# Last wo of a decode attention kernel: the fourth row of every partition is brought ahead of the last v, by four strided transfers to 64 partitions

## The chip, the cores and the metric

The kernel runs on one core of a Trainium2 chip. The metric is the device time of one execution in microseconds, as the median of several runs. Engines are named as the profile names them: PE (matmul, with PEld for its weight loads), DVE (vector), ACT (scalar), POOL (GpSimd) and SP (the queue that issues nearly all transfers). Behind SP and ACT stand 16 DMA engines that move the bytes.

## The reference

One decode step of a parallel block: with `xn = layernorm(x)` for 8 rows of 512, the output is `x + attention(xn) + mlp(xn)`, in float32.

```python
q = (x @ wq).reshape(B, Sq, Hq, Dh).transpose(0, 2, 1, 3)      # 32 heads of 128
k = jnp.repeat(k_cache, rep, axis=1)                           # 8 kv heads, 8192 keys
scores = jnp.einsum("bhqd,bhkd->bhqk", q, k) * (Dh ** -0.5)
o = jnp.einsum("bhqk,bhkd->bhqd", softmax(scores), v)
attention = o.transpose(0, 2, 1, 3).reshape(B, Sq, Hq * Dh) @ wo   # wo: 4096 x 512
mlp = einsum(mish(xn @ w1 + b1), w2)                               # 512 -> 1792 -> 512
```

K and V caches are 256 MiB each, so nearly all of the time is reading them once.

## The kernel before

**Packs.** The 8 kv heads are taken in 4 pairs (PAIRS) and the 8 batches in pairs, which gives 16 packs p of two batches b. Each (p, b) needs one block of K (`kT`) and one of V, 8 MiB each: 128 partitions of 64 KB. Scores of a pack are computed while V of the pack before is multiplied.

**Places and the queue.** All large loads go through three fixed areas of on-chip memory, `place`: "a" (16 rows of 1024 columns a partition; V, and w1 at the start), "b" (20 such rows; K, at the end V of the last pack's first batch and w2) and "w" (4 rows; wq and wo). `plan` (L114) appends a load to `queue`; `pump` (L103) issues loads from the head of this queue while the area that the next one wants is free, and `release` (L110) frees an area. So the order of loads is the order of the `plan` calls, SP (L121) issues them in that order, and a load that waits holds up all behind it. K alternates between rows 0 to 15 and 4 to 19 of "b" (`up`, L142); the last kT lies in rows 4 to 19.

**wo.** wo is laid out in 4 parts of 2 MB, one for each pair of kv heads: 128 partitions with 4 rows (OR = 4) of 1024 columns, 4 KB a row. The first three are used inside the loop (`outputs`, L530). The last one is used in the tail and is loaded in two halves between the pieces of w2.

**Order of loads at the end** (L175 to L181): V of the last pack, batch 0, to "b"; V of batch 1 to "a", in three quarters and one quarter; then w2 in four pieces to "b", with half of the last wo after the second and after the third piece.

**The tail** (L695 to L721). `merges`, `turning` (L498, a selecting matrix from the identity), `values` (L454, V times probabilities) of batch 0, `gather` (L468), `sums`, `merge` (L484), `add_up` (L545: starts the sum of the final output in PSUM), `keep_busy(4)` (L636: matmuls whose result nobody reads), `values` of batch 1, then `gather`, `down` (L623: w2 products) of the first piece, `merge`, and `turn` (L507). `turn` spreads the heads' outputs with four matmuls (L514) so that partition and row fit the layout of wo, and copies the result from PSUM to `oW` in four copies, by DVE (L528) and ACT (L526) in turn. Then follow, on PE in this order: `down` of the second piece, `last_outputs` (L556) of wo's rows 0 and 1, one `keep_busy` matmul, `down` of the third piece, another, `last_outputs` of rows 2 and 3, `down` of the fourth piece. Each float32 matmul stands in the trace as two records. DVE copies the result (L720) and SP stores it (L721).

The instructions of PE, DVE and POOL run in the order of the code (the loop at L725 pins it). Waits between engines are set by what the instructions read and write. Completion of transfers is counted on eight semaphores that SP's transfers use in turn, so the ninth transfer waits for the landing of the first where nothing has implied this already.

Of the kernel before, what the change touches and what calls it, by code (L numbers as in the profile page):

```python
# [8 lines left out]
F32 = mybir.dt.float32  # L9
# [4 lines left out]
P = 128  # L14
B = 8
# [8 lines left out]
G = 4  # L24
# [3 lines left out]
BW = 1024  # L28
# [10 lines left out]
PAIRS = HKV // 2  # L39
NP = B // PB  # L40
PACKS = PAIRS * NP
R = P // G
HE = P // 2
# [7 lines left out]
KR = DH * 2 * NB // P  # L51
# [12 lines left out]

QR = CC
OR = 4
W1R = 2 * CC * P // P
W2R = G * FT // 2 * FP // P
FAR = 1e38
# [3 lines left out]
def kernel(  # L73
# [12 lines left out]
    nc = tc.nc  # L86
# [3 lines left out]
    work = ctx.enter_context(tc.tile_pool(name="work", bufs=2))  # L90
# [4 lines left out]
    place = {n: const.tile([P, size], F32, name=f"kv{n}") for n, size in sizes.items()}  # L95
    queue = []
    taken, landed = {}, {}

    def rows_of(blocks):

        return blocks.rearrange("j p f -> (j p f)").rearrange("(p f) -> p f", p=P)
# [12 lines left out]
    def plan(what, at, blocks, parts=((0, 1),), lo=0):  # L114

        rows = rows_of(blocks)
        n = rows.shape[1]
        t = place[at][:, lo : lo + n]

        def load(cols):  # L120
            nc.sync.dma_start(t[:, cols], rows[:, cols])  # L121
            return t

        for first, end in parts:
            cols = slice(round(first * n), round(end * n))
            queue.append((what, at, lambda cols=cols: load(cols)))


    sc = const.tile([P, 512], F32, name="sc")
# [7 lines left out]
    def blocks_of(src, p, b):  # L137
        i, k = divmod(p, NP)
        lo = ((k * PB + b) * HKV + 2 * i) * NB
        return src[lo : lo + KN]  # L140
# [10 lines left out]
    def plan_v(p, b, at, parts=((0, 1),)):  # L151
        plan(("v", p, b), at, blocks_of(v, p, b), parts)

    def plan_wq(i):
        plan(("wq", i), "w", wq[i * CC : (i + 1) * CC])

    def plan_wo(i, parts=((0, 1),)):
        plan(("wo", i), "w", wo[i * 4 : i * 4 + 4], parts)


    plan_wq(0)
    plan("w1", "a", w1)
# [4 lines left out]
    for p in range(PACKS):  # L167
        for b in range(PB):
            plan_k(p, b)
            if (p, b) in between:  # L170
                what, i = between[p, b]
                (plan_wq if what == "wq" else plan_wo)(i)
            if p > 0:
                plan_v(p - 1, b, "a")
    plan_v(PACKS - 1, 0, "b")  # L175
    plan_v(PACKS - 1, 1, "a", ((0, 3 / 4), (3 / 4, 1)))
    W2_PARTS = ((0, 2), (2, 4), (4, 6), (6, 7))
    for k, (lo, hi) in enumerate(W2_PARTS):
        plan("w2", "b", w2, ((lo / W2R, hi / W2R),))
        if 0 < k < 3:  # L180
            plan_wo(PAIRS - 1, (((k - 1) / 2, k / 2),))  # L181


    S = psum.tile([P, GK], F32, name="s")
# [5 lines left out]
    ident = const.tile([P, P], F32, name="ident")  # L190
# [29 lines left out]
    aT = const.tile([P, 2 * W2R, Q], F32, name="aT")  # L220
    xw = aT.rearrange("p j q -> p (j q)")[:, : W1R * 2 * B]
    xw = xw.rearrange("p (r t b) -> p r t b", r=W1R, t=2)

    def setup():
# [33 lines left out]

        wide = scratch[:B, 2 * D : 2 * D + W1R * P]
        for t in range(2):  # L260
            nc.gpsimd.tensor_copy(
                wide.rearrange("b (r c t i) -> b r c t i", r=W1R, c=CC, t=2)[:, :, :, t, :],
                xc.rearrange("b (c i r) -> b r c i", c=CC, r=W1R),
            )
# [26 lines left out]
    def setup_w1(wide):  # L291
        for r in range(W1R):
            nc.tensor.transpose(  # L293
                M[:, 64 + r * B : 64 + (r + 1) * B], wide[:, r * P : (r + 1) * P], ident[:B, :B]
            )
        for t in range(2):
            nc.vector.tensor_scalar(
                xw[:, :, t, :],
                M[:, 64 : 64 + W1R * B].rearrange("p (r b) -> p r b", r=W1R),
                half[:, t : t + 1],  # L300
                None,
                op0=ALU.mult,
            )

        nc.gpsimd.memset(pt, 0.0)
# [148 lines left out]
    def values(b, vt, lo=0, hi=ROUNDS):  # L454


        for k in range(lo, hi):
            for c in range(G):
                j = G * k + c
                nc.tensor.matmul(  # L460
                    O[b][Q * c : Q * (c + 1), :],
                    pt[:, b, j % 2, j // 2].rearrange("p t e h -> p (t e h)"),
                    vt[:, W4 * DH * j : W4 * DH * (j + 1)],
                    start=(k == 0),
                    stop=(k == ROUNDS - 1),
                )
# [15 lines left out]
    oT, oW = {}, {}  # L482

    def merge(p, b):  # L484

        i, k = divmod(p, NP)
        at = 168 + b * 2 * REP
        nc.tensor.matmul(M[:, at : at + 2 * REP], OS.pop((p, b)), hsel, start=True, stop=True)  # L488
        if b == PB - 1:
            if k == 0:  # L490
                oT[i] = work.tile([P, 2, REP, B], F32, name="oT")
            nc.vector.tensor_mul(  # L492
                oT[i][:, :, :, k * PB : (k + 1) * PB].rearrange("p e h b -> p (e h) b"),
                M[:, 168 : 168 + PB * 2 * REP].rearrange("p (b r) -> p r b", b=PB),
                RT.pop(p).rearrange("p b e h -> p (e h) b"),
            )

    def turning():  # L498

        tid = work.tile([P, HT * KINDS * P], F32, name="e", bufs=1)[:, : OR * P]  # L500
        tid = tid.rearrange("p (r g i) -> p r g i", r=OR, g=G)
        nc.vector.tensor_copy(
            tid, ident.rearrange("p (i r o) -> p r o i", r=OR, o=1).to_broadcast([P, OR, G, Q])
        )
        return tid

    def turn(i, tid):  # L507


        to = oW[i] = work.tile([P, OR, 2, B], F32, name="oW")  # L510
        o = oT.pop(i).rearrange("p n h b -> p (n h b)")
        cols = 2 * REP * B
        for r in range(OR):
            nc.tensor.matmul(  # L514
                M[:, 256 + r * cols : 256 + (r + 1) * cols],
                tid[:, r].rearrange("p g i -> p (g i)"),
                o,
                start=True,
                stop=True,
            )  # L520
        m = M[:, 256 : 256 + OR * cols].rearrange("p (r j q) -> p j r q", r=OR, j=G)
        for j in range(G):
            rows = slice(Q * j, Q * (j + 1))
            dst = to[rows].rearrange("p r h b -> p r (h b)")
            if i == PAIRS - 1 and j % 2:
                nc.scalar.copy(dst, m[rows, j])  # L526
            else:
                nc.vector.tensor_copy(dst, m[rows, j])  # L528

    def outputs(i, w):  # L530

# [24 lines left out]
    def last_outputs(lo, hi, w):  # L556

        for r in range(lo, hi):
            for h in range(2):
                for g in range(G):  # L560
                    at = r * BW + h * D + g * P
                    nc.tensor.matmul(
                        H[Q * g : Q * g + B, :P],
                        oW[PAIRS - 1][:, r, h, :],
                        w[:, at : at + P],
                        start=False,
                        stop=False,
                    )
# [54 lines left out]
    def down(lo, hi, w):  # L623

        for j in range(2 * lo, 2 * hi):
            for g in range(G):
                at = j * D + g * P
                nc.tensor.matmul(
                    H[Q * g : Q * g + B, :P],
                    aT[:, j, :B],  # L630
                    w[:, at : at + P],
                    start=False,
                    stop=(j == 2 * W2R - 1),
                )

    def keep_busy(n):  # L636

        for k in range(n):
            nc.tensor.matmul(C[0][:Q, :], ones[:, :Q], acc, start=True, stop=True)
# [14 lines left out]
    def merges():  # L654
        for p, b in done:
            merge(p, b)
        done.clear()

    for p in range(PACKS):
        for b in range(PB):  # L660
            k = landed.pop(("k", p, b))

            n = PB * p + b - (p > 0)
# [4 lines left out]
            if b == 0 and p > 0:  # L668
                sums(p - 1, lsel.pop(p - 1))
                if p > 1 and (p - 1) % NP == 0:  # L670
                    turn((p - 1) // NP - 1, turning())
# [7 lines left out]
            if (p, b) in between:  # L679
                what, i = between[p, b]  # L680
# [13 lines left out]

    p = PACKS - 1  # L695
    merges()
    tid = turning()
    values(0, landed["v", p, 0])
    gather(p, 0)
    release(("v", p, 0))  # L700
# [7 lines left out]
    w2_sb, wo_sb = landed["w2"], landed["wo", PAIRS - 1]  # L708
    down(*W2_PARTS[0], w2_sb)
    merge(p, 1)  # L710
    turn(PAIRS - 1, tid)
    down(*W2_PARTS[1], w2_sb)
    last_outputs(0, OR // 2, wo_sb)
    keep_busy(1)
    down(*W2_PARTS[2], w2_sb)
    keep_busy(1)
    last_outputs(OR // 2, OR, wo_sb)
    down(*W2_PARTS[3], w2_sb)
    res = acc[:, :P]
    nc.vector.tensor_copy(res, H[:, :P])  # L720
# [3 lines left out]
    last = {}  # L724
# [54 lines left out]
```

## Time and profile before

| | us |
|---|---|
| median of 3 runs | 1311.42 (1311.21 to 1311.5) |
| profiled execution, its own time | 1311.78 |
| its span, first to last instruction | 1310.0 |
| PE busy, DVE busy, ACT busy | 863.7, 384.0, 111.7 |

The span is what the views of the trace count in; 1.78 us of the profiled execution lie around it. "Busy" is time in which an engine works on an instruction; several engines are busy at once. Rows of the chain of waits read: start, length, what it was spent on. Rows of the timeline read: start, length, engine, line, operation, output <- inputs, count, and in brackets how long the engine had been idle and what released it. Rows of the windows read: stretch, its length, busy time and count of PE, PEld, DVE, ACT and POOL, the granted PE clock, the busy share of the 16 DMA engines, and GB/s.

### The profile page before, as it was taken

Reading aid. Unit: us, or ns where it says so; the run is one execution under the profiler, and the core shown is the slowest. Engines: PE = TensorE matmul, PEld = TensorE weight load, DVE = VectorE, ACT = ScalarE, POOL = GpSimd, SP = SyncE. Lnnn points to the kernel's source line nnn. Section 1 sums busy time; section 2 is a strip of 40 time slices with the busy share of each in tenths; the row PEclk is TensorE's granted clock in tenths of the full one; section 3 lists DMA queues with packets and bytes.
Section 4 is the critical chain, followed back from the end, with each engine's and each line's share of the span. In section 5 each row is a group of like instructions: output and inputs, shape, how many; then the busy total and the mean of one; then the engine's idle time right before and its main releaser. Section 6 shows DMA issues by size and latency. Waiting matters only on the chain.

```text
span 1310.0 us, 10715 instructions
## 1 busy us (share of the span) xinstructions
PE 863.7 (66%) x4776; PEld 281.5 (21%) x4776; DVE 384.0 (29%) x590; ACT 111.7 (9%) x294; POOL 4.8 (0%) x10
## 2 busy tenths in 40 slices
PE   4786556866557765677565686655875666766657
PEld 1221112212112221122111222111221221222113
DVE  7150504205051230521405032052320505114051
ACT  1020101001010100101101010010100101001010
POOL 1000000000000000000000000000000000000000
PEclk9887889878799877898878897788877879878789
DMA  9999999999999999999999999999999999999997
GB/s 404 442 423 441 433 429 430 434 437 429 438 431 431 431 439 427 439 423 441 421 444 423 419 447 431 435 427 437 423 425 434 429 439 423 439 431 435 439 425 331
DMA packets 11591, 561.76 MB, mean 429 GB/s; under 512 B 1293, under 2 KB 1425, under 8 KB 1561
## 3 DMA queue, kind: packets, MB, share of 16 engines
q1 hardware_dynamic: 11520, 561.06, 99.3%
q8 instruction: 37, 0.61, 0.2%
q14 instruction: 10, 0.07, 0.0%
q10 hardware_dynamic: 24, 0.02, 0.0%
HBM read 561.01 MB, written 0.07 MB: 428 GB/s over the span
## 4 chain that ended last, share of the span: by engine, by line
DMA 67%; PE 32%; DVE 1%; issue 0%; SPq 0%; ACT 0%; ACTq 0%
DMA kvb<-in_kT 60%; PE c L353 30%; DMA kva<-in_kT 3%; DMA kvb<-in_w 2%; DMA kvb<-in_v 2%; PE o L581 0%; PE h L312 0%; PE o L460 0%; DMA sc<-in_x 0%; SPq L121 0%; DVE nm L379 0%; PE s L365 0%; DVE qT L340 0%; PE m L293 0%; PE o L575 0%
## 5 line engine op out<-in xcount | busy, mean ns | idle before, releaser
L353 PE MATMUL c<-kvb,qT 128*64 128x512 f32 x1984 | 502.4, 671 | 347.3 <-DMA kvb<-in_kT 345.7
L353 PEld LDWEIGHTS c<-kvb,qT 128*64 128x64 f32 x1984 | 162.0, 155 | 687.6 <-issue 470.4
L460 PE MATMUL o<-kva,pt 128*32 128x512 f32 x1984 | 231.4, 620 | 24.2 <-DMA kva<-in_v 24.2
L379 DVE TENSOR_REDUCE nm<-s 128x1 f32<-128x1024 f32 x16 | 19.6, 1225 | 462.2 <-PE s L365 462.2
L412 DVE STREAM_TRANSPOSE raw<-e 128x2048 f32<-128x2048 f32 x32 | 116.0, 3626 | 14.4 <-ACT e L404 12.7
L360 ACT COPY sc<-c 128x512 f32<-128x512 f32 x32 | 18.8, 586 | 1005.0 <-PE c L353 1005.0
L460 PEld LDWEIGHTS o<-kva,pt 128*32 128x32 f32 x1984 | 65.7, 113 | 179.3 <-issue 136.2
L404 ACT ACTIVATE e<-s,nms 128x512 f32<-128x512 f32 x128 | 86.3, 686 | 126.1 <-DVE nms L393 66.8
L492 DVE TENSOR_TENSOR oT<-m,r 128x16 f32<-128x16 f32 x16 | 2.8, 175 | 229.6 <-PE m L488 229.6
L471 DVE TENSOR_SCALAR os<-o,isel 128x128 f32<-128x128 f32 x32 | 11.1, 348 | 155.4 <-PE o L460 155.4
L430 DVE TENSOR_TENSOR pt<-raw 64x256 f32<-64x256 f32 x128 | 53.6, 418 | 2.0
L365 PE MATMUL s<-sc,csel 64*128 64x512 f32 x128 | 36.1, 641 | 8.4 <-ACT sc L360 8.4
L421 DVE TENSOR_TENSOR raw<-raw 128x1024 f32<-128x1024 f32 x32 | 39.2, 1225 | 1.1
L340 DVE TENSOR_TENSOR qT<-qc,bsel 128x1024 f32<-128x1024 f32 x32 | 37.6, 1218 | 0.0
L473 DVE SCALAR_TENSOR_TENSOR os<-o,isel,os 128x128 f32<-128x128 f32 x96 | 33.7, 351 | 3.4
L404 ACT ACTIVATION_READ_ACCUMULATOR e<-s,nms 128x1 f32 x128 | 26.0, 203 | 0.0
L380 PE MATMUL m<-ident,nm 128*1 128x128 f32 x16 | 4.3, 270 | 21.2 <-DVE nm L379 21.2
L312 PE MATMUL h<-kvw,xnT 128*64 128x512 f32 x64 | 16.2, 654 | 0.0
L488 PEld LDWEIGHTS m<-hsel,os 128*128 128x128 f32 x64 | 9.5, 188 | 29.6 <-issue 23.5
L488 PE MATMUL m<-hsel,os 128*128 128x8 f32 x64 | 12.4, 266 | 4.8 <-DVE os L473 3.3
L353 PE MATMUL c<-kva,qT 128*64 128x512 f32 x64 | 14.0, 593 | 1.6 <-DMA kva<-in_kT 1.6
L323 DVE TENSOR_SCALAR e<-h 128x512 f32<-128x512 f32 x16 | 9.9, 684 | 15.9 <-PE h L312 15.9
(100 smaller groups left out, 171.4 us busy)
## 6 DMA issues: line engine op xcount, KB each, us to landing
kvw<-in_wq SPq DMA_DIRECT2D x4, 2048.0 KB, 29.7
kvw<-in_wo SPq DMA_DIRECT2D x3, 2048.0 KB, 30.7
kva<-in_v SPq DMA_DIRECT2D x1, 6144.0 KB, 27.2
kva<-in_w SPq DMA_DIRECT2D x1, 3584.0 KB, 15.8
kvb<-in_w SPq DMA_DIRECT2D x3, 1024.0 KB, 20.6
kva<-in_v SPq DMA_DIRECT2D x1, 2048.0 KB
kvw<-in_wo SPq DMA_DIRECT2D x2, 1024.0 KB, 24.6
kvb<-in_w SPq DMA_DIRECT2D x1, 512.0 KB
```

The costliest lines, as they stand in the source:

```text
L340: nc.vector.tensor_mul(qT[:, b], qc[:, k * PB + b] .rearrange("p r (o h) -> p r o h", o=1) .to_broadcast([P, KR, KN, REP]), bsel.rearrange ...
L353: nc.tensor.matmul(C[b][HE * c : HE * (c + 1), :], t[:, r], k[:, r * BW + c * 512 : r * BW + (c + 1) * 512], start=(r == order[0]), stop=( ...
L360: nc.scalar.copy(sc, C[b])
L365: nc.tensor.matmul(S[:, c * 512 : (c + 1) * 512], csel[HE * c : HE * (c + 1), b].rearrange("p u b h -> p (u b h)"), sc[HE * c : HE * (c + ...
L379: nc.vector.tensor_reduce(nm, S, axis=AX.X, op=ALU.max, negate=True)
L404: nc.scalar.activation(ex[:, :, s, :], S[:, c * 512 : (c + 1) * 512].rearrange("p (t f) -> p t f", t=HT), AF.Exp, bias=NMS[p][:, s : s + 1 ...
L412: nc.vector.transpose(raw.rearrange("p (m t r) -> p t m r", m=TW, t=HT), ex.rearrange("p t s (q m) -> p t m (s q)", m=TW),)
L421: nc.vector.tensor_add(raw[:, :, :n], raw[:, :, :n], raw[:, :, n:])
L430: nc.vector.tensor_add(pt[rows, b, c].rearrange("p m t e h -> p (m t) e h")[:, :, e], raw[rows, :, at : at + REP], raw[rows, :, V8 + at : ...
L460: nc.tensor.matmul(O[b][Q * c : Q * (c + 1), :], pt[:, b, j % 2, j // 2].rearrange("p t e h -> p (t e h)"), vt[:, W4 * DH * j : W4 * DH * ...
L473: nc.vector.scalar_tensor_tensor(os, O[b][:, DH * i : DH * (i + 1)], isel[:, i : i + 1], os, op0=ALU.mult, op1=ALU.add,)
L488: nc.tensor.matmul(M[:, at : at + 2 * REP], OS.pop((p, b)), hsel, start=True, stop=True)
```

## The change

Of the last wo, rows 0 to 2 of every partition are loaded as before to "w" (now as two rows and one row). Row 3 of every partition, 128 x 4 KB, goes to the rows of "b" that the last V does not use (rows 16 to 19, `OX_AT`), ahead of V of the last pack's batch 1. There it lies on 32 of the first 64 partitions: for k = 0 to 3 one transfer writes partitions k, 8 + k, ..., 56 + k, each with four rows that come from four source partitions. POOL clears the area first, since half of its 64 partitions are not written. `turning(True)` gives the selecting matrix for row 3 the matching order of partitions, and `turn` writes `oW` for the last pair into `sc`, with 3 + 4 rows, by one copy more. `last_outputs` takes 64 partitions for rows 3 to 6. The two single `keep_busy` matmuls of the tail go.

```diff
+OM = OR - 1
+OX = OM + G
+OE = HE // 8
+OK = R // OE
...
+    OX_AT = KR * BW
+
+    def plan_last_wo():
+        rows = rows_of(wo[(PAIRS - 1) * 4 :]).rearrange(
+            "(j e k) (r f) -> k r e j f", e=OE, k=OK, r=OR
+        )
+        t = place["b"][:HE, OX_AT : OX_AT + G * BW]
+
+        def load():
+            nc.gpsimd.memset(t, 0.0)
+            for k in range(OK):
+                nc.sync.dma_start(t[k::8].rearrange("e (j f) -> e j f", j=G), rows[k, OM])
+            return t
+
+        queue.append(("last wo", "behind b", load))
...
     plan_v(PACKS - 1, 0, "b")
+    plan_last_wo()
     plan_v(PACKS - 1, 1, "a", ((0, 3 / 4), (3 / 4, 1)))
+    WO_PARTS = ((0, 2), (2, 3))
...
-            plan_wo(PAIRS - 1, (((k - 1) / 2, k / 2),))
+            lo, hi = WO_PARTS[k - 1]
+            plan_wo(PAIRS - 1, ((lo / OR, hi / OR),))
...
+        if last:
+
+            own = tid[:, OM].rearrange("p g i -> p (g i)")
+            nc.vector.memset(own, 0.0)
+            nc.vector.tensor_copy(
+                own[:, :HE].rearrange("p (e k) -> p e k", e=OE)[:, :, :OK],
+                ident.rearrange("p (e k r) -> p e k r", e=OE, k=OK)[:, :, :, OM],
+            )
...
+        n = OM if last else OR
         for j in range(G):
...
+        if last:
+            dst = to[:HE, OM:].rearrange("p j h b -> p j (h b)")
+            nc.vector.tensor_copy(dst, m[:HE, :, OM])
...
         for r in range(lo, hi):
+            n = P if r < OM else HE
...
-                        oW[PAIRS - 1][:, r, h, :],
-                        w[:, at : at + P],
+                        oW[PAIRS - 1][:n, r, h, :],
+                        w[:n, at : at + P],
...
-    last_outputs(0, OR // 2, wo_sb)
-    keep_busy(1)
+    wx_sb = place["b"][:, OX_AT - OM * BW :]
+    last_outputs(OM, OM + 2, wx_sb)
+    last_outputs(*WO_PARTS[0], wo_sb)
+    last_outputs(OM + 2, OX, wx_sb)
     down(*W2_PARTS[2], w2_sb)
-    keep_busy(1)
-    last_outputs(OR // 2, OR, wo_sb)
+    last_outputs(*WO_PARTS[1], wo_sb)
     down(*W2_PARTS[3], w2_sb)
```

More of the change, by code (lines that the diff above doesn't have):

```diff
@@ L496, in merge, with turning @@
             )
-    def turning():
+    def turning(last=False):
         tid = work.tile([P, HT * KINDS * P], F32, name="e", bufs=1)[:, : OR * P]
@@ L504, in turning @@
         )
+        if last:
[5 more added lines that the diff above has]
+            )
         return tid
     def turn(i, tid):
-        to = oW[i] = work.tile([P, OR, 2, B], F32, name="oW")
+        last = i == PAIRS - 1
+        if last:
+            to = sc[:, : OX * 2 * B].rearrange("p (r h b) -> p r h b", r=OX, h=2)
+        else:
+            to = work.tile([P, OR, 2, B], F32, name="oW")
+        oW[i] = to
         o = oT.pop(i).rearrange("p n h b -> p (n h b)")
@@ L521, in turn @@
         m = M[:, 256 : 256 + OR * cols].rearrange("p (r j q) -> p j r q", r=OR, j=G)
+        n = OM if last else OR
         for j in range(G):
             rows = slice(Q * j, Q * (j + 1))
-            dst = to[rows].rearrange("p r h b -> p r (h b)")
-            if i == PAIRS - 1 and j % 2:
-                nc.scalar.copy(dst, m[rows, j])
-            else:
-                nc.vector.tensor_copy(dst, m[rows, j])
+            dst = to[rows, :n].rearrange("p r h b -> p r (h b)")
+            if last and j % 2:
+                nc.scalar.copy(dst, m[rows, j, :n])
+            else:
+                nc.vector.tensor_copy(dst, m[rows, j, :n])
+        if last:
+            dst = to[:HE, OM:].rearrange("p j h b -> p j (h b)")
+            nc.vector.tensor_copy(dst, m[:HE, :, OM])
     def outputs(i, w):
@@ L696 @@
     merges()
-    tid = turning()
+    tid = turning(True)
     values(0, landed["v", p, 0])
```

## The prediction

> **What bounds the kernel now.** I read the page first, for which resource is full, then the chain of work that ended last over the last 65 us, and then the last ten microseconds in the timeline and in short windows.
>
> ```profile
> span 1310.0 us, 10715 instructions
> ...
> DMA packets 11591, 561.76 MB, mean 429 GB/s; under 512 B 1293, under 2 KB 1425, under 8 KB 1561
> ## 3 DMA queue, kind: packets, MB, share of 16 engines
> q1 hardware_dynamic: 11520, 561.06, 99.3%
> q8 instruction: 37, 0.61, 0.2%
> ...
> q10 hardware_dynamic: 24, 0.02, 0.0%
> ```
>
> The 16 DMA engines are full: the loads on q1 alone take 99.3% of their time. No compute engine can be the limit before the tail, and bytes can't be saved, because the change moves the same 2 MB of wo. One engine moves 429 / 16 = 26.8 GB/s, so 32 KB on one engine is 32768 / 26.8 = 1.22 us and 64 KB is 2.44 us. These two numbers carry the forecast.
>
> ```profile
> 1247.64 25.68 DMA kvb<-in_v
> ...
> 1278.20 0.33 SPq L121
> ...
> 1278.57 1.21 SPq L121
> ...
> 1279.82 26.57 DMA kvb<-in_w
> 1306.39 0.04 issue
> 1306.43 0.67 PE h L628 x16
> 1307.10 0.02 issue
> 1307.12 0.29 DVE acc L720
> ```
>
> The end is set by the last piece of w2. It landed at 1306.39, and 16 matmul records, a copy and the store follow. It was issued 26.57 us earlier, so its issue is not late: it stood in the DMA engines' queues.
>
> ```profile
> 1301.00:1302.00 1.00, 1.00 (x18) 0.32 (x6) 0.00 (x0) 0.00 (x0) 0.00 (x0) 1.00 0.94 385
> 1302.00:1303.00 1.00, 0.50 (x13) 0.28 (x16) 0.00 (x0) 0.00 (x0) 0.00 (x0) 1.00 0.73 303
> 1303.00:1303.50 0.50, 0.50 (x29) 0.50 (x21) 0.00 (x0) 0.00 (x0) 0.00 (x0) 1.00 0.49 205
> 1303.50:1304.00 0.50, 0.50 (x13) 0.21 (x2) 0.00 (x0) 0.00 (x0) 0.00 (x0) 1.00 0.55 205
> 1304.00:1304.50 0.50, 0.50 (x2) 0.00 (x0) 0.00 (x0) 0.00 (x0) 0.00 (x0) 1.00 0.32 131
> 1304.50:1305.00 0.50, 0.12 (x1) 0.00 (x0) 0.00 (x0) 0.00 (x0) 0.00 (x0) 1.00 0.22 90
> 1305.00:1305.50 0.50, 0.32 (x12) 0.32 (x16) 0.00 (x0) 0.00 (x0) 0.00 (x0) 1.00 0.28 115
> 1305.50:1306.00 0.50, 0.50 (x28) 0.46 (x19) 0.00 (x0) 0.00 (x0) 0.00 (x0) 1.00 0.06 25
> ```
>
> These rows say what is wrong with the tail (the last two columns are the busy share of the 16 DMA engines and GB/s; before them the granted clock, 1.00). All loads have the same bytes per engine, yet the engines do not stop together. Share times 16 is the number still busy: 15 after 1301, about 8 from 1303 to 1304, four or five until 1305.5, then one. So about eight engines are through by 1303.25, four more by about 1304.5, and four run to 1305.9. The work left after 1301 is (0.94 + 0.73 + 0.5 x (0.49 + 0.55 + 0.32 + 0.22 + 0.28 + 0.06)) = 2.63 us of all engines: shared evenly it would be done at 1303.6, not 1305.9. No balancing of this tail can give more than 2.3 us.
>
> **The change part by part.** *Which engines carry what.* The fourth rows of wo are 128 x 4 KB = 512 KB. Before, 16 engines take 32 KB of it each, in the tail. After, four transfers of 8 rows bring it, ahead of the last v. If a transfer of 8 rows goes to 8 engines, those carry 64 KB of it and the others nothing. For the end that is +1.22 us on the loaded eight and -1.22 us on the other eight. The page supports 8 engines for 8 rows: q10 carries only x (8 rows) and b1 (4 rows), and its 24 packets are 12 rows and 12 more, as many as one completion write for each engine used if these are 8 and 4.
>
> [...]
>
> *Which engines are late.* If the loaded eight are those through by 1303.25, they end at 1304.5, the four last ones at 1304.7, and the tail is level: -1.2 us. If one of the middle four (up to 1304.5) is loaded, it ends at 1305.7: -0.2 us. I take the middle of the two, **-0.7 us**. The views name no engine, so this is a choice. One hint is the instruction traffic on q8: 37 packets that are not spread like the data can put some engines behind the others, and followed packet by packet they seem to fall on the same engines that are late; the four last ones do not seem to be among the eight that carried x. That is a reading of chains of packets, not a row, and I put no more than odds of about three to one on it.
>
> *Memset and four issues on SP, ahead of the last v.*
>
> ```profile
> 1234.44 16.59 PE L353 MATMUL c<-kvb,qT 128*64 128x512 f32 x64 [10.60 <-DMA kvb<-in_kT]
> 1247.64 0.33 SPq L121 DMA_DIRECT2D kvb<-in_v  x1
> 1260.69 2.04 SPq L121 DMA_DIRECT2D kva<-in_v  x2
> 1277.53 0.42 SPq L121 DMA_DIRECT2D kvw<-in_wo  x1
> ```
> ```profile
> L305 POOL MEMSET pt<- 128x2048 f32 x1 | 1.8, 1837 | 1.2 <-PE m L293 1.2
> ```
>
> The memset overwrites the last rows of the last kT, which the scores read until 1234.44 + 16.59 = 1251.03. A memset of 2048 elements took 1837 ns, so 4096 take 3.7 us, to 1254.7. SP then issues the four: by the rows one costs 0.33 to 1.21 us, so 1.3 to 4.9 us, done by 1259.6. SP's next, the last v, waited until 1260.69 anyway for its place. So SP's queue is not pushed back, with a margin of 1 us. If the cover goes, nothing is lost for another 12 us, as the DMA engines work on the v that was issued at 1247.64 and landed 25.68 us later, at 1273.3. Cost: nothing. In the built program SP also waits for each of these four to land before it reuses its semaphore, first at the issue of wo (1277.53). They land by 1273.3 + 2.44, say 1276: no delay. If each took twice as long, that issue would slip by about a microsecond, in a queue whose last data arrive 27 us later: nothing.
>
> *The last v.*
>
> ```profile
> 1287.91 4.69 PEld L460 LDWEIGHTS o<-kva,pt 128*32 128x32 f32 x48 [0.46 <-DMA kva<-in_v]
> ```
>
> It stands behind the four. Loaded engines reach it 2.44 us later. They are also the early ones in my case, about 2.7 us ahead of the last (1303.25 against 1305.9), so its landing, for which PE waited (0.46 us), hardly moves. If a middle engine is loaded, up to 1 us of it shows here as well as at the end; both run side by side, so it is not added.
>
> *Compute in the tail.*
>
> ```profile
> 1282.50 0.35 DVE L471 TENSOR_SCALAR os<-o,isel 128x128 f32<-128x128 f32 x1 [8.03 <-PE o L460]
> ...
> 1298.57 1.06 PE L628 MATMUL h<-kvb,aT 128*8 128x128 f32 x32
> 1299.16 0.22 DVE L528 COPY oW<-m 32x64 f32<-32x64 f32 x1 [0.27 <-ACT oW L526]
> 1299.42 0.20 ACT L526 COPY oW<-m 32x64 f32<-32x64 f32 x1 [0.29 <-DVE oW L528]
> 1300.33 1.06 PE L562 MATMUL h<-kvw,oW 128*8 128x128 f32 x32 [0.70 <-DMA kvw<-in_wo]
> 1302.72 1.06 PE L628 MATMUL h<-kvb,aT 128*8 128x128 f32 x32 [0.50 <-DMA kvb<-in_w]
> 1305.18 1.06 PE L562 MATMUL h<-kvw,oW 128*8 128x128 f32 x32 [0.56 <-DMA kvw<-in_wo]
> 1306.43 0.62 PE L628 MATMUL h<-kvb,aT 128*8 128x128 f32 x16 [0.19 <-DMA kvb<-in_w]
> ```
>
> The last wo's products go from 32 matmuls (64 records, 2.12 us) to 24 + 32 = 56 (112 records, 3.7 us). 64 rows in place of 128 are not shown by the trace; I take the same 33 ns a record, as columns are equal, with 0 and twice as bounds. One copy more (0.22 us) follows the four of oW: they end at 1299.9 instead of 1299.62. PE then has no wait: first extra products 1299.95 to 1301.0, wo's first half to 1302.1, rest of the extra ones to 1303.1, w2's third piece (landed before 1302.72) to 1304.2, the last 8 matmuls of wo to 1304.75. The last w2 piece lands at 1306.39 - 0.7 = 1305.7, in the level case 1305.2. So the 1.6 us of products fit where PE used to wait and run the two removed keep_busy matmuls, with 0.4 to 0.9 us to spare. At twice the price a record for the extra 64 (2.1 us more) PE reaches its last group at 1306.85 instead of 1306.43, and the gain turns into +0.4 us. The two small DVE operations for the selecting matrix come in the 8.03 us for which DVE waits ahead of 1282.50: nothing.
>
> **Sum.** 0 (memset, SP) + 0 (PE) - 0.7 (last landing). The profiled execution took 1311.78 us, its span 1310.0 and 1.78 around it; it becomes 1311.1. The median is 0.36 us below that execution, so I forecast 1310.7.
>
> **Rivals.** *One: two engines share a way into SBUF (slower).* Each of the four transfers writes partitions 8 apart. If pairs of the eight engines then meet on one way in, each gets half of 26.8 GB/s: 4.88 us instead of 2.44. The loaded engines end at 1303.25 + 1.22 + 2.44 = 1306.9, and the end moves by +1.0 us: 1312.4. It decides as soon as the four cost a loaded engine over 2.7 + 1.22 = 3.9 us in all. For it: nothing in the trace shows eight engines writing this pattern. [...]
>
> [...]
>
> *Two: a loaded engine is among the last four.*
>
> ```profile
> q8 instruction: 1, 0.02, 0.6%
> ```
>
> Its 1.22 us comes on top of 1305.9: +1.2 us, 1312.6. For it: the row, from the DMA view of 1295 to 1306, shows an instruction packet on one engine amid the last transfers, and PE's stream grows there (24 matmuls more at two records and two weight loads each, less the two keep_busy), so that a packet can hold up another engine than now. Against: the hint above.
>
> *Three: the four transfers do not do what is said* and spread over all 16 engines. Then each engine has the same bytes as before: 1311.4, if PE's extra products fit. Against it: q10's count.
>
> *Four: one and two together.* An engine that is among the last four is loaded, and slow on its way in: 1.22 + 2.44 = +3.7 us, 1315.1.
>
> **How the numbers follow.** Forecast 0.43 (own range 1310.0 to 1311.3, the level case and the middle engine); rival one 0.25; two 0.15; three 0.06; four 0.08; something that gains more 0.03. About 0.2%, 2.6 us, is what a measurement of this kernel can tell from no change. Only rival four passes it, with a little of rival one if the four cost still more: slower 0.10. A gain of 2.6 us would exceed the 2.3 us of perfect balance: faster 0.03. Within 0.2%: 0.87. The range leaves out the upper end of rival four and the very low end: 1310.0 to 1313.0.
>
> **What would show it.** Right: in windows over the last 5 us the DMA share falls steeply from about 0.9 to 0, instead of stepping through 0.5 and 0.25; w2's last piece lands about 0.7 us earlier; the new products sit where PE waited; the last v is issued at the same time. Rival one: the four transfers land clearly later after the v than 2.4 us, the last v lands later and PE's wait for it grows. Two: the staircase remains, and ends later. Three: the staircase remains as it is. Wrong altogether: SP issues the last v late, or PE has no wait left before its last group.

## The result and the profile after

After: 1318.76 us, the median of 6 runs (1317.23 to 1321.11), against 1311.47 us (1311.21 to 1311.52, 6 runs) before. The ratio is 1.0057, with an interval of 1.0044 to 1.007: 0.6% longer, and clear of the noise. The profiled execution took 1317.23 us, with 1.83 us around its span. It is the fastest of the six, so its trace shows 5.4 us of a change that is 7.3 us by the medians.

The page of the kernel after, the rows of the span and of the data:

```profile
span 1315.4 us, 10817 instructions
...
DMA packets 11750, 561.76 MB, mean 427 GB/s; under 512 B 1324, under 2 KB 1456, under 8 KB 1848
q1 hardware_dynamic: 11680, 561.06, 99.3%
```

The packets bear out that each transfer runs on eight engines: q1 has 160 more than before (11680 against 11520), which is 128 pieces of 4 KB and 32 packets of 4 bytes, eight for each transfer. Before, q1 has 1280 packets of 4 bytes for its 80 transfers, 16 each, so I read them as one completion write for each engine used (with one transfer of 128 rows, below, there are 128 + 16 more). That the four use the same eight engines is assumed here and below; no view names an engine, and "engine e" stands for the one that carries row e of a transfer. The bytes are the same, the DMA engines are as busy as before (99.3%), and yet the span is 5.4 us longer. So the engines did not stand idle; they moved the same bytes more slowly at some place. Windows of 4 us over the stretch in which the four transfers and the two last V's move find it. Before (the last two columns are the DMA share and GB/s):

```profile
1262.00:1266.00 4.00, 0.73 (x6) 0.30 (x2) 3.81 (x9) 2.79 (x8) 0.00 (x0) 1.00 0.87 377
1266.00:1270.00 4.00, 0.00 (x0) 0.00 (x0) 3.88 (x3) 0.00 (x0) 0.00 (x0) 0.64 1.02 442
1270.00:1274.00 4.00, 0.54 (x4) 0.23 (x8) 3.83 (x10) 0.00 (x0) 0.00 (x0) 0.50 0.93 401
1274.00:1278.00 4.00, 4.00 (x28) 1.09 (x24) 0.47 (x1) 0.00 (x0) 0.00 (x0) 0.58 1.00 430
1278.00:1282.00 4.00, 4.00 (x44) 1.18 (x36) 0.00 (x0) 0.00 (x0) 0.00 (x0) 1.00 1.13 483
```

And after:

```profile
1262.00:1266.00 4.00, 0.82 (x7) 0.30 (x2) 3.82 (x9) 2.79 (x8) 0.00 (x0) 1.00 1.02 442
1266.00:1270.00 4.00, 0.00 (x0) 0.00 (x0) 3.88 (x3) 0.00 (x0) 0.00 (x0) 0.69 1.07 340
1270.00:1274.00 4.00, 0.00 (x0) 0.00 (x0) 3.82 (x10) 0.00 (x0) 0.00 (x0) 0.50 1.00 193
1274.00:1278.00 4.00, 1.06 (x8) 0.46 (x12) 0.91 (x4) 0.00 (x0) 0.00 (x0) 0.50 0.95 219
1278.00:1282.00 4.00, 4.00 (x27) 0.95 (x20) 0.00 (x0) 0.00 (x0) 0.00 (x0) 0.60 0.90 375
```

From 1270 to 1278 the DMA share stays at about 1.0 while the rate falls to 193 and 219 GB/s. A busy share of 1 at half the rate means packets that take twice as long: packets of v of 64 KB, 2.42 us in the median before, take up to 5.07 us. Over the 20 us shown the mean rate is 314 GB/s instead of 427, which loses 20 x (1 - 314/427) = 5.3 us, against 5.4 us by which the span is longer. So nearly all of it is lost here; I call this stretch the dip.

The dip also says that not only the eight loaded engines suffer. The other eight alone, at 26.8 GB/s each (429 / 16, from before), would move 214 GB/s, and the loaded ones something more. The measured rate of all sixteen is 193.

Where it reaches the end: the timeline of SP and POOL of the kernel after,

```profile
1247.73 0.33 SPq L127 DMA_DIRECT2D kvb<-in_v  x1
1254.74 2.69 SPq L177 DMA_DIRECT2D kvb<-in_wo  x4
1260.78 2.04 SPq L127 DMA_DIRECT2D kva<-in_v  x2
1278.92 2.03 SPq L127 DMA_DIRECT2D kvb<-in_w  x2
```
```profile
1251.20 3.51 POOL L175 MEMSET kvb<- 64x4096 f32 x1 [1238.54 <-PE c L378]
```

The first products with V of batch 0 and, in the kernel after, with V of batch 1 (the first row is before, the other two are after):

```profile
1273.46 8.97 PE L460 MATMUL o<-kvb,pt 128*32 128x512 f32 x64 [7.98 <-DMA kvb<-in_v]
```
```profile
1276.94 9.15 PE L485 MATMUL o<-kvb,pt 128*32 128x512 f32 x64 [11.36 <-DMA kvb<-in_v]
1294.22 8.77 PE L485 MATMUL o<-kva,pt 128*32 128x512 f32 x64 [2.20 <-DMA kva<-in_v]
```

SP issued the last v at 1260.78, as before (1260.69); nothing was late on a queue up to there. V of batch 0 landed late: PE's products with it start at 1276.94, where they started at 1273.46 before. The chain of waits then goes through the last v:

```profile
1260.78 33.40 DMA kva<-in_v
...
1294.22 8.81 PE o L485 x64
...
1306.38 0.99 PE h L672 x32
1307.37 0.28 issue
1307.66 3.03 PE h L606 x96
1310.69 0.99 PE h L672 x32
1311.68 0.44 PE h L606 x16
1312.12 0.48 PE h L672 x16
...
1312.62 0.29 DVE acc L765
```

Its first part landed at 1260.78 + 33.40 = 1294.18, 6.3 us later than before (PE's weight loads with it started at 1287.91). From there to the end the chain holds PE and DVE and no DMA. PE had waited 2.20 us for this v, and the granted clock was 0.71 from 1294 to 1296 and 0.50 from 1296 to 1298, where it was 1.00 before; the products with it took 8.77 us instead of 7.31. The last w2 is not what the end waits for in this execution: the windows of the last three microseconds of data,

```profile
1308.00:1309.00 1.00, 1.00 (x44) 0.78 (x36) 0.00 (x0) 0.00 (x0) 0.00 (x0) 1.00 0.63 258
1309.00:1310.00 1.00, 1.00 (x44) 0.77 (x36) 0.00 (x0) 0.00 (x0) 0.00 (x0) 1.00 0.23 82
1310.00:1311.00 1.00, 1.00 (x44) 0.78 (x36) 0.00 (x0) 0.00 (x0) 0.00 (x0) 1.00 0.06 25
```

show the engines run dry at about 1311, some 5 us later than before (1305.9), and PE takes up the last piece at 1312.12. The staircase from 0.63 to 0.23 and 0.06 is still there. So the dip delays both ways to the end by 5 to 6 us, and which of them ends last differs between executions: in the profiled one of the kernel "source 16 KB apart" below it is w2 again, which lands at 1284.18 + 28.50 = 1312.68.

### The profile page after: what moved, and what is told of

The parts are those of the page before. It is cut to its first block, busy times and chain, and to the rows that moved or that the text cites. A ratio compares the mean times of both kernels' runs of the same rounds, so it can differ in the third digit from the quotient of the medians.

```text
span 1315.4 us, 10817 instructions
## 1 busy us (share of the span) xinstructions
PE 865.7 (66%) x4820; PEld 280.8 (21%) x4820; DVE 385.0 (29%) x593; ACT 111.7 (8%) x294; POOL 8.3 (1%) x11
## 3 DMA queue, kind: packets, MB, share of 16 engines
q1 hardware_dynamic: 11680, 561.06, 99.3%
## 4 chain that ended last, share of the span: by engine, by line
DMA 57%; PE 38%; DVE 5%; issue 1%; ACT 0%; ACTq 0%; DVEq 0%
DMA kvb<-in_kT 52%; PE c L378 31%; PE o L485 4%; DMA kva<-in_kT 3%; DMA kva<-in_v 3%; DVE raw L437 1%; DVE pt L455 1%; DVE nm L404 1%; PE s L390 1%; PE o L625 0%; PE h L337 0%; DVE os L498 0%; DVE raw L446 0%; ACT sc L385 0%; PE h L606 0%
## 5 line engine op out<-in xcount | busy, mean ns | idle before, releaser
L485 PE MATMUL o<-kva,pt 128*32 128x512 f32 x1984 | 234.4, 627 | 25.0 <-DMA kva<-in_v 24.9
L485 PE MATMUL o<-kvb,pt 128*32 128x512 f32 x64 | 9.1, 734 | 11.4 <-DMA kvb<-in_v 11.4
```

What stands on the lines that cost most here:

```text
L485: nc.tensor.matmul(O[b][Q * c : Q * (c + 1), :], pt[:, b, j % 2, j // 2].rearrange("p t e h -> p (t e h)"), vt[:, W4 * DH * j : W4 * DH * ...
```

## The experiments

Read packet by packet (the four transfers are 128 packets of 4 KB), a piece takes 159 ns in the quickest case (the median in the kernels below that have no dip); in the kernel after the median is 331 ns and all of them sum to 44.8 us, in the mean 5.6 us for each of eight engines. So the question was what makes a 4 KB piece, and everybody else's packets with it, slow: where it reads (the source rows, 64 KB apart for neighbouring rows of a transfer), where it writes (the partitions), that only eight engines run, or the moved quarter itself. The kernels below change one of these at a time, and in the selecting matrix, the copy and the products what follows from it. Each ratio is to runs of the kernel before on the same chip; their medians were 1311.37 to 1311.62 us.

| kernel | median, us | ratio to before (interval) | 4 KB piece, median |
|---|---|---|---|
| source in one piece | 1318.12 | 1.0053 (1.0037 to 1.007) | 334 ns |
| source 16 KB apart | 1318.76 | 1.0051 (1.0036 to 1.0066) | 344 ns |
| partitions 4e + k | 1313.43 | 1.0013 (1.0004 to 1.0023) | 159 ns |
| sixteen engines | 1311.96 | 1.0001 (0.9992 to 1.0011) | 159 ns |
| 12 apart | 1315.86 | 1.0036 (1.0022 to 1.0049) | 281 ns |
| 2 apart | 1315.94 | 1.0039 (1.0026 to 1.0052) | 289 ns |
| partitions 64 + 4e + k | 1318.03 | 1.0047 (1.0033 to 1.006) | 322 ns |
| partitions 32 + 4e + k | 1312.91 | 1.001 (1.0001 to 1.002) | 159 ns |
| 4e + k, 256 KB more, same source | 1315.17 | 1.0031 (1.002 to 1.0043) | 226 ns |
| 4e + k, 256 KB more, other source | 1314.52 | 1.0022 (1.0012 to 1.0032) | 159 ns |

**The source.** The first kernel gets the fourth rows as an input of their own, laid out so that a transfer reads 128 KB in a row; the second keeps wo and lets neighbouring rows of a transfer lie 16 KB apart.

```diff
-                nc.sync.dma_start(t[k::8].rearrange("e (j f) -> e j f", j=G), rows[k, OM])
+                nc.sync.dma_start(t[k::8].rearrange("e (j f) -> e j f", j=G), wx[k].rearrange("j e f -> e j f"))
```
```diff
-            "(j e k) (r f) -> k r e j f", e=OE, k=OK, r=OR
+            "(j k e) (r f) -> k r e j f", e=OE, k=OK, r=OR
```

> The same 512 KB of wo come from an array of their own, laid out so that each transfer reads 128 KB in a row (eight engines 4 KB apart, pieces of 4 KB as before); destination, memset, products unchanged; nothing is left out. Theory D (destination: engines meet on a way into SBUF): the four transfers stay slow, 250 to 500 ns a 4 KB piece, DMA rate near 200 GB/s for 8 us, 1317 to 1320 us. Theory S (source: all eight engines read 64 KB apart, at the same place of their 64 KB, and this slows the memory for everyone): the rate stays near 430 GB/s, the last v's first part lands near 1288.5, time 1310.0 to 1311.5. Theory N (eight engines with few pieces are slow by themselves): as D.

> The same four transfers to the same partitions, but the eight engines of a transfer read rows 16 KB apart instead of 64 KB (source order j k e instead of j e k, selecting matrix to match); nothing is left out. Theory D and N: unchanged, 1317 to 1320 us. Theory S: the eight engines no longer read at one place of their 64 KB, the dip shrinks at least by half, 1310.5 to 1314 us.

Windows of the first and of the second kernel:

```profile
1270.00:1274.00 4.00, 0.00 (x0) 0.00 (x0) 3.82 (x10) 0.00 (x0) 0.00 (x0) 0.50 1.02 200
1274.00:1278.00 4.00, 0.87 (x6) 0.27 (x10) 0.47 (x3) 0.00 (x0) 0.00 (x0) 0.50 0.98 222
```
```profile
1270.00:1274.00 4.00, 0.00 (x0) 0.00 (x0) 3.82 (x10) 0.00 (x0) 0.00 (x0) 0.50 1.06 185
1274.00:1278.00 4.00, 0.67 (x4) 0.23 (x8) 0.55 (x3) 0.00 (x0) 0.00 (x0) 0.50 1.00 196
```

The dip is the same with either source. Where the pieces come from does not make it.

**The partitions.** Transfer k writes partitions 4e + k, in 0 to 31, instead of 8e + k; the selecting matrix, the copy and the products follow (32 partitions).

```diff
+OP = OE * OK
...
-                nc.sync.dma_start(t[k::8].rearrange("e (j f) -> e j f", j=G), rows[k, OM])
+                nc.sync.dma_start(t[k::OK].rearrange("e (j f) -> e j f", j=G), rows[k, OM])
```

> The four transfers write partitions k, 4 + k, ..., 28 + k (32 partitions in a row, none skipped) instead of 8 apart; selecting matrix and products to match; source and pieces unchanged; nothing is left out. [...] Theory S: the source is the same, the dip stays, 1317 to 1320 us. Theory N: the dip stays.

Its windows, and its last landing in the chain of waits:

```profile
1270.00:1274.00 4.00, 0.85 (x5) 0.26 (x9) 3.67 (x11) 0.00 (x0) 0.00 (x0) 0.50 1.05 448
1274.00:1278.00 4.00, 4.00 (x24) 1.12 (x20) 0.00 (x0) 0.00 (x0) 0.00 (x0) 0.51 1.10 471
...
1305.00:1306.00 1.00, 0.87 (x32) 0.77 (x32) 0.00 (x0) 0.00 (x0) 0.00 (x0) 1.00 0.13 53
1306.00:1307.00 1.00, 0.81 (x24) 0.34 (x16) 0.00 (x0) 0.00 (x0) 0.00 (x0) 1.00 0.07 29
```
```profile
1279.21 28.36 DMA kvb<-in_w
...
1307.62 0.67 PE h L673 x16
```

No dip, and every piece takes 159 to 171 ns, though source, bytes and number of transfers are those of the kernel after. 5.3 of the 7.3 us are gone by a change of the target partitions alone. The time of before is not reached all the same. What stays, 1.9 us by the medians, is something else: the last w2 lands at 1279.21 + 28.36 = 1307.57, 1.2 us after the 1306.39 of before, on two engines, then one (0.13 and 0.07 of 16), that still work when the rest are through.

**Sixteen engines.** Row 3 of all 128 partitions by one plain transfer ahead of the last v, with the products of before (32 matmuls); the single keep_busy matmuls go as in the change.

```diff
-            nc.gpsimd.memset(t, 0.0)
-            for k in range(OK):
-                nc.sync.dma_start(t[k::8].rearrange("e (j f) -> e j f", j=G), rows[k, OM])
+            nc.sync.dma_start(t, rows[:, OM * BW :])
```

> Row 3 of all 128 partitions is brought ahead of the last v by one plain transfer of 128 pieces of 4 KB, to row 16 of the same area; products as before the change (32 matmuls on 128 partitions), the two single keep_busy matmuls left out; no part of the result is left out. All engines carry 32 KB of it. Theories D, S and N: no dip, each engine has the bytes of the kernel before, 1311.0 to 1311.8 us, the staircase at the end as before. If moving the quarter ahead of the last v is itself the cost, 1314 us or more.

```profile
1270.00:1274.00 4.00, 0.81 (x4) 0.23 (x8) 3.72 (x9) 0.00 (x0) 0.00 (x0) 0.50 1.10 452
...
1303.00:1304.00 1.00, 0.12 (x6) 0.12 (x9) 0.00 (x0) 0.00 (x0) 0.00 (x0) 1.00 0.61 250
1304.00:1305.00 1.00, 0.94 (x32) 0.65 (x24) 0.00 (x0) 0.00 (x0) 0.00 (x0) 1.00 0.38 143
1305.00:1306.00 1.00, 0.62 (x16) 0.34 (x16) 0.00 (x0) 0.00 (x0) 0.00 (x0) 1.00 0.13 53
```

No dip, the staircase of before, and the time of before (ratio 1.0001; the median is 0.4 us above that of before, and 0.2 us above the range expected). Bringing a quarter of wo ahead of the last v has no cost or gain of its own that these runs can tell.

**Which partitions.** Two conjectures on the cause were left: pairs of the eight engines meet on one way in (the prediction's rival one), or an engine that writes partitions which another engine fills in the plain loads slows both. No view shows ways in, or which engine fills which partitions. What three kernels can tell is which partitions have the dip: 12 apart, 2 apart, and 4 apart from partition 64.

```diff
+OD = 12
...
-                nc.sync.dma_start(t[k::8].rearrange("e (j f) -> e j f", j=G), rows[k, OM])
+                nc.sync.dma_start(t[k::OD].rearrange("e (j f) -> e j f", j=G), rows[k, OM])
```
```diff
-                nc.sync.dma_start(t[k::8].rearrange("e (j f) -> e j f", j=G), rows[k, OM])
+                at = 16 * (k // 2) + k % 2
+                nc.sync.dma_start(t[at : at + 15 : 2].rearrange("e (j f) -> e j f", j=G), rows[k, OM])
```
```diff
+OB = slice(HE, HE + OP)
...
-        t = place["b"][:HE, OX_AT : OX_AT + G * BW]
+        t = place["b"][OB, OX_AT : OX_AT + G * BW]
...
-                nc.sync.dma_start(t[k::8].rearrange("e (j f) -> e j f", j=G), rows[k, OM])
+                nc.sync.dma_start(t[k::OK].rearrange("e (j f) -> e j f", j=G), rows[k, OM])
```

> [...] Theory O (each engine has partitions of its own, those that it writes in a 128-partition load, and whoever writes elsewhere also holds up the owner): a dip like the changed kernel's or somewhat less, pieces of 300 ns and more, 1315 to 1320 us. Theory W (the wide spread as such is slow): as O, or worse.

> 32 partitions in a row again, but the eight engines of a transfer write 2 apart (two engines in each group of four partitions); selecting matrix to match; nothing is left out. [...] Theory W: close together is good, no dip, 1312 to 1314 us.

> Partitions 4 apart as in the second experiment, but from 64 on (64 + k, 68 + k, ..., 92 + k); products take these 32 partitions; nothing is left out. [...] Theory W: no dip.

One window each, in this order:

```profile
1270.00:1274.00 4.00, 0.00 (x0) 0.00 (x0) 3.86 (x7) 0.00 (x0) 0.00 (x0) 0.50 0.94 260
```
```profile
1270.00:1274.00 4.00, 0.00 (x0) 0.00 (x0) 3.82 (x10) 0.00 (x0) 0.00 (x0) 0.50 1.05 249
```
```profile
1270.00:1274.00 4.00, 0.00 (x0) 0.00 (x0) 3.83 (x9) 0.00 (x0) 0.00 (x0) 0.50 1.00 216
```

All three dip, 12 and 2 apart less deeply than the kernel after (260 and 249 against 193 GB/s, pieces of 281 and 289 ns; for 12 apart 300 ns and more were expected). A wide spread is not what it takes, since 2 apart dips; and 4 apart is not by itself what saves, since it dips from partition 64 (216 GB/s, pieces of 322 ns). It remained possible that simply the first 32 partitions are free of it. So the same 4 apart were put into 32 to 63. The difference from the kernel with partitions 64 + 4e + k:

```diff
-OB = slice(HE, HE + OP)
+OB = slice(OP, 2 * OP)
```

> Like the run with partitions 4e + k, but in partitions 32 to 63: engine e writes 32 + 4e + k. No other size changes. [...] Rival 'only the first 32 partitions are free': a dip to about 200 GB/s, last v at about 1294, time 1317 to 1319. If it dips, the slow extra pieces in the run with more load on the eight came from their place, and not from their source.

```profile
1270.00:1274.00 4.00, 1.32 (x8) 0.46 (x12) 3.73 (x11) 0.00 (x0) 0.00 (x0) 0.50 0.99 395
1274.00:1278.00 4.00, 4.00 (x24) 1.12 (x20) 0.12 (x1) 0.00 (x0) 0.00 (x0) 0.50 1.05 446
```
```profile
1279.44 26.95 DMA kvb<-in_w
```

No dip, and the last w2 lands at 1279.44 + 26.95 = 1306.39, as before. The rate is not there at once: the window from 1266 to 1270 has 317 GB/s, at a share of 0.75. The pieces take 159 ns in the median and 24.1 us in sum; 28 of the 128 take 205 to 418 ns, as 17 of those with sixteen engines take 211 to 324 ns, so a few slow pieces do not make a dip. Partitions 0 to 31 and 32 to 63 are free of it when row e of transfer k goes to the one numbered 4e + k among them; every other choice tried dips.

**The load on eight engines.** Here two more transfers of eight rows bring 256 KB to partitions 32 + 4e + k, and no product reads them: 32 KB more for each of the eight engines if these are the same, an estimated 1.2 us at the end (32768 / 26.8) if one of them finishes last. The first of the two kernels reads the same rows as two of the four transfers, the second other rows of wo.

```diff
+            more = place["b"][OP : 2 * OP, OX_AT : OX_AT + G * BW]
+            for k in range(2):
+                nc.sync.dma_start(more[k::OK].rearrange("e (j f) -> e j f", j=G), rows[k, OM])
```

In the second kernel the last line reads `rows[k + 2, 0]`.

> The second experiment (partitions 4 apart from 0) plus two more transfers of 128 KB to partitions 32 to 63 that nobody reads: 32 KB more on each of the eight loaded engines, nothing on the others; nothing is left out. If loaded engines are the last at the end of the second experiment (my second rival), everything ends 1.2 us later than there: 1314.0 to 1315.2 us, and its staircase ends 1.2 us later. If its last engines are others, or PE, the time stays within 0.3 us of 1313.4.

> As the run with 256 KB more on the same eight engines, that no product reads, but the 256 KB come from other rows of wo than those the four transfers read at the same time. If the extra pieces were slow because two transfers read the same rows: pieces of 159 ns now, and the time is the four's (1313.4) plus 1.2 us for 32 KB more on each of eight engines, 1314.2 to 1315.0, if those engines are the last to finish; 1313.4 if they are not, since they'd have 1.2 us to spare. If the partitions 32 to 63 were the cause: pieces stay at 200 to 470 ns, time 1315 to 1317.

The row of the chain of waits that sets the end, of the first and of the second, and SP's timeline of the second:

```profile
1279.51 30.48 DMA kvb<-in_w
```
```profile
1262.04 28.49 DMA kva<-in_v
```
```profile
1254.29 3.01 SPq L178 DMA_DIRECT2D kvb<-in_wo  x4
1257.35 1.38 SPq L181 DMA_DIRECT2D kvb<-in_wo  x2
1262.04 11.78 SPq L128 DMA_DIRECT2D kva<-in_v  x2
```

In the first the last w2 lands at 1309.99, 2.4 us after that of 4e + k, and the time is 1.7 us longer. But many pieces were slow (156 to 471 ns, the rate 290 GB/s from 1270 to 1274) while v's 64 KB packets kept to 2.42 to 2.67 us, so the surplus is not only load. The second kernel settles that: with another source all 192 pieces take 159 to 172 ns. Reading the same rows twice at about the same time was slow, not the partitions. Its time, 1.1 us above 4e + k, has the predicted size, yet its chain ends through the last v (first part landed at 1262.04 + 28.49 = 1290.53) and not through w2: PE had waited 2.53 us for it, the granted clock was 0.57 and 0.58 from 1290 to 1294, and the products with it took 8.59 us. And SP's two issues of that v stretch over 11.78 us instead of 2.04. With six transfers ahead of it, its second part is the ninth in the turn of the eight semaphores and waits until V of batch 0 has landed; it comes some 10 us late, in the first kernel too (12.52 us). So neither kernel prices the load alone; this test stays inconclusive.

## Why the prediction was wrong

**The step that failed** is the one that priced the four transfers: "those carry 64 KB of it and the others nothing", at 2.44 us, and from it that the last v's "landing, for which PE waited (0.46 us), hardly moves". It moved by 6.3 us, PE's wait for it grew to 2.20 us, and the time came to 1318.76 us where 1310.7 was forecast. The pieces took 44.8 us in sum, 5.6 us for each of eight engines, and all sixteen engines moved 193 and 219 GB/s meanwhile, where the unloaded eight alone would move 214 at 26.8 GB/s each.

**Rival one** had the place and the sign right: 4.88 us on a loaded engine, against 5.6 measured. But it charged this to the loaded engines only, which had 2.7 us to spare, and so came to +1.0 us. Its cause, pairs that meet on one way in, is shown by no run: the dip comes at 8, 12 and 2 apart, and at 4 apart from partition 64 but not from 0 or 32. Rival four came nearest in time (1315.1), by the same price and the same confinement to the loaded engines. Rival three is refuted by the count of packets: eight packets of 4 bytes a transfer, where one of 128 rows has 16.

That the target partitions decide is shown by six placements, two free (159 ns a piece) and four slow (281 to 331 ns). What sets the two apart from the four is not shown: that an engine holds up others when it writes partitions that they fill was the author's conjecture, and the views name no engine. Why the rate of all sixteen falls under what the unloaded eight would move (193 against 214 GB/s) stays open: no run here separates a shared way from a stall that spreads backwards, and none writes to these partitions while v's load is not running beside it.

**Which engines are late.** The forecast took the loaded eight for the early ones, or at worst with a middle one among them, -0.7 us, and gave rival two (+1.2 us) a third of that chance. The hint behind the forecast, that the late engines did not seem to be among those that carried x, tells of the loaded ones only if all transfers of eight rows use the same eight engines, which no run shows. Without the dip the change would still have missed that gain: 4e + k is 1.9 us and 32 + 4e + k 1.3 us above before. In the profiled execution of the former the last landing is exactly rival two's +1.2 us; in that of the latter it is where it was before (1306.39); there the span is that of before too (1309.9 us), and 3.0 of its 1312.93 us lie around it. Their runs spread over 1312.17 to 1315.22 and 1311.18 to 1315.57, those with sixteen engines over 1311.76 to 1312.41. So with eight engines loaded more than the others the end came later in the median and less steadily. That the late engines are loaded ones is argued from the size of the shift, not shown.

**What held.** The memset took 3.51 us (3.7 forecast) and ended at 1254.71; SP's four issues took 2.69 us (1.3 to 4.9 forecast) and ended at 1257.43, before SP's wait for the last v's place was over, and that v was issued on time. Later SP did slip, w2's issues by 3.5 us (1278.92 against 1275.45), but the last w2 was not what the end waited for. The products cost what a record costs with 128 rows: the 96 records from 1307.66 took 3.03 us, 32 ns each, and 64 of them have 64 rows. They fit where PE used to wait in the kernel without the dip: there the last group still waits for w2. In the profiled execution of the kernel after, PE sets the end from the last v on, because its v came 6.3 us late, w2's last data only some 5 us, and the products with that v ran at a lower clock (8.77 us against 7.31).

## What to carry to other kernels

In this kernel a transfer to a few partitions could not be priced by bytes per engine alone. Before sending strided pieces beside a plain load, measure the placement: here a piece took 159 ns at 4e + k and 32 + 4e + k, and 281 to 331 ns at four others; if no placement is free, one plain transfer over 128 partitions was so here (ratio 1.0001). Even at the two free placements the transfers to eight engines left the time 1.3 to 1.9 us longer. Read the DMA share and the GB/s together: here a share of 1.0 at half the rate was time lost inside the packets, and no idle DMA engine points to it.

## What the runs showed of the hardware

- With 4 KB pieces written 8, 12 or 2 partitions apart, or 4 apart from partition 64, beside the load of v, all sixteen engines moved 185 to 260 GB/s from 1270 to 1274, and pieces took 281 to 344 ns in the median. With the same pieces 4 apart from partition 0 or 32: 448 and 395 GB/s, 159 ns in the median. Before, without them: 401 GB/s.
- Distance alone does not decide: 8 apart gave 1318.76 us, 12 apart 1315.86, 2 apart 1315.94, 4 apart 1313.43, 1312.91 or 1318.03, depending on where it begins (partition 0, 32 or 64).
- With two more transfers that read the same 4 KB rows at about the same time, pieces took up to 471 ns; with other rows 159 to 172 ns (one trace each).
- Matmuls with 64 or 32 rows in place of 128 took the same 32 to 33 ns a record.
- After a wait of 2.20 us PE's granted clock was 0.71 and then 0.50 in windows of 2 us, and the products of the last v took 8.77 us instead of 7.31; after 1.18 us (sixteen engines) it was 1.00 throughout, and they took 7.08 us. A wait of 2.76 us (256 KB more, same source) was followed by 7.07 us, so the length of the wait alone does not tell.
